# Linear attention plus gated MLP on one core: stage-by-stage kernel rewritten as one recorded plan for five engines

## The chip, the core and the metric

The kernel runs on one core of a Trainium2 chip. A core has TensorE (PE, matrix products; PEld is its weight load), VectorE (DVE), ScalarE (ACT), GpSimd (POOL) and SyncE (SP, which issues DMA). TensorE writes its results into PSUM; the other engines fetch them there. Both kernels divide PSUM into banks of 512 float32 columns, and the changed one uses eight.

The metric is device time in microseconds (us), lower is better. The kernel before took 369.79 us (median of all its 16 runs). The span of a profile is about 2 us less than the time of the same run. With one core there is no second die to compare with; all profiled runs quoted here are of the state "fast".

## The reference

x is 2048 tokens by 640. It is normalised once (xn); an attention block and a gated MLP both read xn, and x plus both is the output.

```python
xn = layernorm(x)
# A: 32 heads of 20; phi = [softmax(u), softmax(-u)] over the 20 features
q, k, v = split(xn @ wqkv)
phi_q, phi_k = phi(q @ w_phi), phi(k @ w_phi)
kv  = sum over tokens of phi_k^T v ;  z = sum over tokens of phi_k
o   = (phi_q @ kv) / (phi_q @ z + 1e-6)
A   = o @ wo
# B
h   = silu(xn @ w1) * (xn @ w3)          # 640 -> 1536
B   = h @ w2
return x + A + B
```

Every query needs the finished sum over all tokens, so A has a barrier in the middle. B (gate/up products, then output products) has none: it needs only xn. That freedom is what the change uses.

## The kernel before

Both kernels first fuse wq and wk with w_phi (transposes, then small products). The kernel before then does one stage after the other; the tile framework orders instructions inside a stage.

```python
nc.gpsimd.memset(vaug[:], 0.0)                 # 12096 columns
nc.gpsimd.memset(vaug[:, :, :, 120:126], 1.0)
... fuse wq, wk with w_phi (TensorE transposes, ScalarE copies) ...
for t in range(NST):                           # 16 tiles: all statistics first
    bn_stats, bn_stats, bn_aggr                # VectorE
rstd = ...                                     # one Sqrt for all 16 tiles
for t in range(NST): xn = ...; 5 transposes; copy to xnT
for t in range(NST): K and V products, exp, sums, reciprocals, phik, vaug
for g in range(NG): ... 16 KV products per group and sign ...
for sc in range(NSC):                          # 4 chunks of 512 tokens
    for g in range(NG):   pq = ...; eqp = exp(pq); eqm = exp(-pq)
    for tau in range(4):  rt, tt products; copies to r_sb, t_sb
    for fi in range(KF):                       # 12 gate/up blocks
        gp = 5 products; up = 5 products       # "bank_d"/"bank_e", "bank_f"
        th = tanh(gp / 2); up_sb = up / 2                        # ScalarE
        gs = (th + 1) * gp                                       # VectorE
        nc.gpsimd.tensor_mul(out=hT[:, fi, :], in0=gs[:], in1=up_sb[:])
    m1, m2, den, rinv, cB, cA                  # VectorE, attention arithmetic
    om1 = r * cB; om2 = t * cA; o = om1 + om2  # VectorE, 2880 columns each
    for tau in range(4):  transpose o -> oT
    for ti in range(4):   acc = hT @ w2 + oT @ wo; res = acc + xr; store
```

The softmax here doesn't subtract the row's maximum and nothing guards it: scores larger than these inputs give would overflow.

## Time and profile before

| | before |
|---|---|
| time, median | 369.79 us |
| span of the profile | 365.9 us |
| TensorE matmuls, columns | 2134, about 668,400 |
| columns / 2.4 GHz + 2.5 ns per matmul | about 284 us |
| span minus that | about 82 us |

The last rows need one reading: five back-to-back matmuls of 512 columns take 1.08 us in the chain of waits, 216 ns each, and sixteen of 126 columns take 0.88 us (their starts, 105.74 to 106.62 us), 55 ns each. Both are the columns / 2.4 GHz plus about 2.5 ns. Multiply out the code and one has an estimate of the time that TensorE needs at this pace without a pause, called its floor below. TensorE's "busy" is not that number, because the ends of matmuls are modelled.

The page's first two parts for the kernel before: busy time per engine, then forty slices of 9.1 us with the busy share in tenths.

```profile
PE 311.0 (85%) x2134; PEld 173.2 (47%) x2134; DVE 167.7 (46%) x294; ACT 175.5 (48%) x300; POOL 129.4 (35%) x93
...
PE   0006677999989999979999989999997999998885
...
PEclk9999969999999999989999999999999999999899
```

TensorE's row begins with three zeros and reaches 9 only in the eighth slice, and the clock row has a 6 in the sixth: TensorE had paused. The timeline of the first 60 us says why (start, duration, engine, line, operation, output<-inputs, count, in brackets the idle time before and what ended it).

```profile
8.89 1.28 DVE L166 BATCH_NORM_STATS2 stats<-xall 128x6 f32<-128x320 bf16 x3 [8.89 <-DMA xall<-in_A_x_dram]
...
9.79 10.20 POOL L115 MEMSET vaug<- 128x12096 bf16 x1
...
10.94 11.09 DVE L110 COPY selj<-ident 20x20 bf16<-20x20 bf16 x6
...
30.37 1.29 PE L141 MATMUL pwT<-ident,wq 128*120 128x128 bf16 x10 [0.42 <-DVE wphi L131]
...
48.24 6.11 PE L196 MATMUL pst<-ident,xn 128*128 128x128 bf16 x55 [2.20 <-DVE xn L186]
...
58.68 1.24 PE L219 MATMUL pk<-wkphi,xnT 128*128 128x512 bf16 x5 [1.35 <-ACT xnT L201]
```

At 9.79 us GpSimd starts to clear vaug for 10.2 us; VectorE's six small copies (20 columns each) take 11.09 us in that time, and the statistics behind them wait. The first fusion transpose is at 30.37 us, the first transpose of xn at 48.24, the first K product at 58.68.

The chain that ended last, as shares of the span by engine and by line:

```profile
PE 54%; POOL 12%; DVE 12%; issue 3%; ACT 2%; POOLq 1%; ACTq 0%
POOL hT L388 12%; PE acc L445 12%; PE gp L365 10%; PE up L373 10%; PE pq L331 8%; PE acc L453 6%; DVE sp L257 3%; DVE sm L260 3%; DVE phik_p L267 3%; PE kvp L294 3%; PE rt L345 2%; PE tt L355 2%; PE pot L433 1%; DVE rcm L266 1%; DVE res L46
```

Only 54% of what decided the end is TensorE. The largest single line is GpSimd's product hT. The timeline of the end of the first chunk:

```profile
145.68 12.95 POOL L388 TENSOR_TENSOR hT<-gs,up_sb 128x512 bf16<-128x512 bf16 x5 [0.89 <-ACT up_sb L383]
145.69 3.15 DVE L405 TENSOR_TENSOR om<-r_sb,cB 128x2880 bf16<-128x2880 bf16 x1
...
150.50 3.49 DVE L410 TENSOR_TENSOR om<-t_sb,cA 128x2880 bf16<-128x2880 bf16 x1
...
155.63 1.99 DVE L416 TENSOR_TENSOR o<-om,om 128x2880 bf16<-128x2880 bf16 x1
...
157.68 0.45 PE L433 MATMUL pot<-ident,o 128*128 128x128 bf16 x5 [1.76 <-DVE o L416]
```

Five hT products take 12.95 us there; alone one takes 1.15 us (the median of all 48). They run beside VectorE's three long attention products. The transposes of o wait for the last of these, and the output products for both.

### The profile page before, as it was taken

The page shows a single profiled execution, that of the slowest core. Times are in us where ns is not written, and L with a number is a line of the kernel's source. Part 1 is how long each engine was busy: PE and PEld are TensorE (multiplying, and loading weights), DVE is VectorE, ACT ScalarE, POOL GpSimd, SP SyncE. Part 2 cuts the span into 40 slices and gives each one's busy share as a digit, 9 for nine tenths or more (in the row PEclk, how much of TensorE's full clock was granted, in tenths as well). Part 3 has the DMA queues.
Part 4 walks back from the last instruction along what each step waited for, and adds up shares of the span by engine and source line. Part 5 has one row for each costly group of instructions (what it writes and reads, how often), then busy time and mean ns, then how long its engine had stood idle before and what let it go on. Part 6 is the DMA issues. An engine that isn't in the chain of part 4 may idle for free.

```text
span 365.9 us, 5348 instructions
## 1 busy us (share of the span) xinstructions
PE 311.0 (85%) x2134; PEld 173.2 (47%) x2134; DVE 167.7 (46%) x294; ACT 175.5 (48%) x300; POOL 129.4 (35%) x93
## 2 busy tenths in 40 slices
PE   0006677999989999979999989999997999998885
PEld 0005564555577445445545435554544554543442
DVE  0998072999962125921112780211394210279111
ACT  0006988877721777431177632237753216863300
POOL 7930000666630224930023690012386002359100
PEclk9999969999999999989999999999999999999899
DMA  8998000000010000002110001110000211000011
GB/s 246 370 390 289 2 0 3 0 2 0 3 39 2 0 0 2 1 0 73 37 37 0 2 0 36 56 53 3 1 0 2 68 42 36 2 0 0 27 47 36
DMA packets 13233, 17.39 MB, mean 48 GB/s; under 512 B 1690, under 2 KB 11930, under 8 KB 13210
## 3 DMA queue, kind: packets, MB, share of 16 engines
q1 hardware_dynamic: 9552, 13.76, 11.3%
q10 hardware_dynamic: 3274, 3.30, 2.8%
q8 instruction: 16, 0.26, 0.3%
q0 software_dynamic: 384, 0.01, 0.1%
q14 instruction: 7, 0.06, 0.1%
HBM read 14.44 MB, written 2.62 MB: 47 GB/s over the span
## 4 chain that ended last, share of the span: by engine, by line
PE 54%; POOL 12%; DVE 12%; issue 3%; ACT 2%; POOLq 1%; ACTq 0%
POOL hT L388 12%; PE acc L445 12%; PE gp L365 10%; PE up L373 10%; PE pq L331 8%; PE acc L453 6%; DVE sp L257 3%; DVE sm L260 3%; DVE phik_p L267 3%; PE kvp L294 3%; PE rt L345 2%; PE tt L355 2%; PE pot L433 1%; DVE rcm L266 1%; DVE res L463 1%
## 5 line engine op out<-in xcount | busy, mean ns | idle before, releaser
L388 POOL TENSOR_TENSOR hT<-gs,up_sb 128x512 bf16<-128x512 bf16 x48 | 83.8, 1758 | 150.6 <-ACT up_sb L383 144.9
L385 DVE SCALAR_TENSOR_TENSOR gs<-th,gp 128x512 bf16<-128x512 bf16 x48 | 32.8, 684 | 76.3 <-ACT th L381 72.6
L365 PE MATMUL gp<-xnT,w 128*128 128x512 bf16 x240 | 64.9, 380 | 0.6 <-DVE gs L385 0.5
L373 PE MATMUL up<-xnT,w 128*128 128x512 bf16 x240 | 63.7, 380 | 0.0
L445 PE MATMUL acc<-w,hT 128*128 128x512 bf16 (+1 forms) x384 | 60.2, 302 | 4.1 <-DVE res L463 2.7
L338 ACT ACTIVATE eqp<-pq 120x512 bf16<-120x512 f32 (+1 forms) x24 | 14.3, 596 | 70.6 <-PE pq L331 70.6
L463 DVE TENSOR_TENSOR res<-acc,xr 128x640 bf16<-128x640 f32 x16 | 13.2, 824 | 75.4 <-PE acc L453 75.4
L445 PEld LDWEIGHTS <-hT 128*128 128x128 bf16 x384 | 31.7, 100 | 30.2 <-issue 3.7
L272 POOL TENSOR_TENSOR phik_m<-ekm,rcm 128x640 bf16<-128x640 bf16 x16 | 26.1, 1631 | 43.7 <-PE vp L244 28.8
L383 ACT ACTIVATE up_sb<-up 128x512 bf16<-128x512 f32 x48 | 28.8, 600 | 18.0 <-POOL hT L388 10.2
L373 PEld LDWEIGHTS <-w 128*128 128x128 bf16 x240 | 22.3, 98 | 24.3 <-issue 0.4
L365 PEld LDWEIGHTS <-w 128*128 128x128 bf16 x240 | 22.0, 98 | 24.7 <-issue 3.0
L381 ACT ACTIVATE th<-gp 128x512 bf16<-128x512 f32 x48 | 28.7, 599 | 8.1 <-PE gp L365 7.9
L331 PE MATMUL pq<-xnT,wqphi 128*120 128x512 bf16 (+1 forms) x120 | 30.3, 379 | 0.8 <-DVE kvr_m L305 0.4
L453 PE MATMUL acc<-wo,oT 128*128 128x512 bf16 (+1 forms) x160 | 29.9, 315 | 0.0
L166 DVE BATCH_NORM_STATS2 stats<-xall 128x6 f32<-128x320 bf16 x32 | 23.5, 773 | 8.9 <-DMA xall<-in_A_x_dram 8.9
L126 PE MATMUL pwp<-wps,selj 20*120 20x120 bf16 (+1 forms) x6 | 1.3, 270 | 28.7 <-DVE stats L166 22.1
L219 PE MATMUL pk<-wkphi,xnT 128*128 128x512 bf16 x80 | 19.9, 379 | 1.4 <-ACT xnT L201 1.4
L436 ACT COPY oT<-pot 128x640 bf16<-128x640 bf16 x16 | 11.1, 692 | 20.6 <-PE pot L433 20.6
L236 PE MATMUL vp<-wv,xnT 128*128 128x512 bf16 x80 | 19.9, 379 | 0.0
L331 PEld LDWEIGHTS <-wqphi 128*120 128x120 bf16 (+1 forms) x120 | 14.4, 127 | 11.0 <-issue 3.0
L453 PEld LDWEIGHTS <-oT 128*128 128x128 bf16 x160 | 13.3, 101 | 8.7 <-issue 1.1
(85 smaller groups left out, 413.9 us busy)
## 6 DMA issues: line engine op xcount, KB each, us to landing
w<-in_B_w_dram SPq DMA_DIRECT2D x3, 1920.0 KB, 24.0
xall<-in_A_x_dram SPq DMA_DIRECT2D x2, 1280.0 KB, 11.5
xr<-in_A_x_dram SPq DMA_DIRECT2D x16, 160.0 KB, 2.3
out_dram<-res SPq DMA_DIRECT2D x16, 160.0 KB, 1.8
wq<-in_A_wqkv_dram ACTq DMA_DIRECT2D x1, 800.0 KB, 10.1
wk<-in_A_wqkv_dram ACTq DMA_DIRECT2D x1, 800.0 KB, 14.9
wv<-in_A_wqkv_dram ACTq DMA_DIRECT2D x1, 800.0 KB, 21.5
wo<-in_A_wo_dram ACTq DMA_DIRECT2D x1, 800.0 KB, 25.4
```

Source lines behind the costliest of these rows:

```text
L166: nc.vector.bn_stats(out=stats[:, t, i, :], in_=xall[:, t, i * 320 : (i + 1) * 320])
L219: nc.tensor.matmul(pk[:, 0:512], xnT[:, c, t * P : (t + 1) * P], wkphi[:, c, 0:512], start=(c == 0), stop=(c == KD - 1),)
L272: nc.gpsimd.tensor_mul(out=phik_m[:, t, :].rearrange("p (h d) -> p h d", d=Dh), in0=ekm[:].rearrange("p (h d) -> p h d", d=Dh), in1=rcm[:, ...
L331: nc.tensor.matmul(pq[:gw, :], wqphi[:, c, 120 * g : 120 * g + gw], xnT[:, c, s0 : s0 + 512], start=(c == 0), stop=(c == KD - 1),)
L365: nc.tensor.matmul(gp[:, :], w1[:, c, fi * P : (fi + 1) * P], xnT[:, c, s0 : s0 + 512], start=(c == 0), stop=(c == KD - 1),)
L373: nc.tensor.matmul(up[:, :], w3[:, c, fi * P : (fi + 1) * P], xnT[:, c, s0 : s0 + 512], start=(c == 0), stop=(c == KD - 1),)
L381: nc.scalar.activation(out=th[:], in_=gp[:], func=AF.Tanh, scale=0.5)
L383: nc.scalar.activation(out=up_sb[:], in_=up[:], func=AF.Copy, scale=0.5)
L385: nc.vector.scalar_tensor_tensor(out=gs[:], in0=th[:], scalar=1.0, in1=gp[:], op0=ALU.add, op1=ALU.mult)
L388: nc.gpsimd.tensor_mul(out=hT[:, fi, :], in0=gs[:], in1=up_sb[:])
L445: nc.tensor.matmul(acc[:, n0:n1], hT[:, fi, ti * P : (ti + 1) * P], w2[:, fi, n0:n1], start=(fi == 0), stop=False,)
L453: nc.tensor.matmul(acc[:, n0:n1], oT[:, c, ti * P : (ti + 1) * P], wo[:, c, n0:n1], start=False, stop=(c == KD - 1),)
```

## The change

The intent: keep TensorE at work from the first data to the last, with gate/up blocks of B wherever A would leave it idle. The rewrite is nearly total; this is its core.

```diff
-stage after stage, order inside a stage left to the tile framework
+class Plan:              # operations are recorded with engine, guessed duration, dependencies,
+    def run(self): ...   # buffers; TensorE and allocations keep the recorded order, the other
+                         # engines may take any of their next 80 operations that is ready first
+ringp = tile_pool(bufs=6, PSUM)          # one ring of six banks for everything but KV
+kva, kvb                                 # two banks that collect KV, tile by tile
-x in two loads of 1.3 MB; some weights on another queue at the same time
+x tiles 0 to 3 in four loads, then wv, a quarter of w1/w3, wk, ... in order of need
-nc.gpsimd.memset(vaug[:], 0.0)           # 12096 columns
+vaug: four small tiles, only the columns of ones set
-statistics of all 16 tiles, then one rstd
+statistics, rstd, xn per pair of tiles, ahead of use
+16 warm-up matmuls on the first x tile
+def fill(us): issue gate/up blocks until so many us of TensorE work have been added
+for t in range(16):
+    K(t); fill(1.6); V(t); fill(1.6); T(t + 4); KV(t - 2); part of the wq fusion
-6 Q groups of 120 rows, last of 40       # 5 groups of 128
-attention arithmetic per chunk (2880 columns), then its transposes
+RT(0); RT(1); ATT(0); fill(2.2)
+for i in range(8):                       # pairs of tiles, 1280 columns
+    RT(2*i + 2); RT(2*i + 3)             # next pair
+    OT(2*i); OT(2*i + 1)                 # this pair's transposes (for i = 0 after Q, not before)
+    ATT(i + 1)                           # next pair's arithmetic, VectorE
+    fill(4.4); every other pair: Q of the next chunk
+    O(2*i); O(2*i + 1)                   # this pair's output products and store
-hT on GpSimd for all 48 blocks           # GpSimd for 40, VectorE for 8
```

RT is the product of exp(q) with the KV sums, ATT the attention arithmetic, OT the transposes of its result, O the output products.

## The prediction

> **What bounds the kernel now.** TensorE, but in three pieces with gaps. The timeline has almost no matmul before 30 us: VectorE's first read of x ends its wait at 8.9 us, and from 10.9 us a statistics instruction and a copy stand for 11 us behind GpSimd's 10.2 us clearing of vaug. The weight fusion's first transpose is at 30.4 us, the normalised x transposes at 48.2 to 57 us, the first K product at 58.7 us. K/V (58.7 to 104 us) runs at 2.7 us a tile, TensorE at 98% and VectorE nearly as full (windows view). The KV sums take 105 to 115 us. Then four 512-row chunks take 60 us each (the last ends at 366). Within a chunk the chain of waits passes three times to GpSimd's hT product (12% of the span in all), whose 12 multiplies (1.76 us each) hold the output matmuls back, and to the attention tail before the oT transposes.
>
> **TensorE's own floor.** Five 512-column matmuls take 1.08 us in the chain of waits, i.e. columns/2.4 GHz + 2.5 ns. The Trainium skill ("TensorE: Matmul & The Clock Gate", "Wait — 56ns, not 53.3ns?") gives the same sum; the trace agrees. Counting columns from the code: before 668,600 columns in 2134 matmuls = 284 us; after 655,800 in 2092 = 278.5 us. So the change removes only 5 us of TensorE work (Q in 5 full groups instead of 6, narrower KV products), and even pays 16 warm-up matmuls. It must earn its gain by filling about 80 us of idle or waiting TensorE.
>
> **What moves.** x comes in 160 KB pieces, first in the queue; the 10 us clearing is gone; normalisation is per tile; gate/up products serve as filler in the fusion, K/V and attention stages from one six-bank PSUM ring; KV accumulates tile by tile; each engine's order is fixed by a planner.
>
> **Other engines, estimated from traced durations.** VectorE about 200 us in all. In K/V, per tile: K about 2.7, statistics 0.86, xn 0.45, copy from PSUM about 0.5, gates about 1.0 us: 5.5 us against 6.6 us of TensorE work. ScalarE about 160 us, GpSimd about 105 us. None exceeds TensorE, but VectorE has little slack in K/V.
>
> **The sum.**
> - First data about 3.5 us (a 160 KB load lands in 2.3 us in the list of DMA issues).
> - Cold clock in the warm-up: 2 us (the windows view shows 0.5 granted at 48 to 52 us).
> - TensorE work 278.5 us, plus 2 for 84-column products limited by weight loads, plus 1 for clock.
> - Waits 15 us: about 1 us for each of eight attention pairs, because eight short RT groups (0.17 us of matmul each) fill six banks faster than ScalarE copies them (about 0.42 us); the rest in the fusion, K/V, and the change to attention.
> - Tail 4 us: add and output load.
> - Outside the span 2 us (367.8 against 365.9).
>
> Total 308 us: 0.83 of before. Range 297 to 321. Faster by over 2%: 0.97; within 2%: 0.02; slower: 0.01.
>
> **What would show each step.** First matmul at 3 to 5 us, first V product near 9 us; matmuls starting nearly without gaps from there; the hT product gone from the chain of waits; TensorE at over 85% of the chain; TensorE idle behind ScalarE's copies of RT; granted clock at 0.98 or more; the 11 us VectorE stall gone.
>
> **What would make it wrong.** VectorE and GpSimd blocking each other in K/V, where xn copies and GpSimd products now overlap (10 to 20 us more). Weight loads in 768-byte rows arriving late, so that early filler waits. VectorE standing in order behind the last x piece, queued behind all weights (about 33 us). A lower granted clock once TensorE is dense. On the other side, if the six-bank ring hides the copies, 297 us.

## The result, and the profile after

| | before | after |
|---|---|---|
| time, median | 369.79 us | 297.05 us (296.55 to 297.52, 11 runs) |
| span of the profile | 365.9 us | 294.6 us |
| span minus TensorE's floor | about 82 us | about 16 us |

The ratio is 0.8039 (95% interval 0.8012 to 0.8067). It is the mean time of one kernel's fast runs over that of the other's in the same rounds, so not quite the ratio of the medians above. The output is correct.

The same lines of the page after the change (slices are now 7.4 us):

```profile
PE 285.3 (97%) x2092; PEld 176.9 (60%) x2092; DVE 192.7 (65%) x341; ACT 144.7 (49%) x316; POOL 94.2 (32%) x115
...
PE   5899999899999999999999999999999999999995
...
PEclk9999999999999999999999999999999999999999
```

TensorE is at 9 in all but four slices (the first two, the eighth and the last); the clock row has no dip. The chain that ended last:

```profile
PE 84%; DVE 9%; ACT 3%; issue 2%; DMA 1%
PE bank L505 29%; PE bank L741 18%; PE bank L339 13%; PE bank L745 7%; PE bank L593 6%; PE bank L636 3%; DVE stats L253 2%; DVE ks L387 2%; PE bank L712 2%; PE kva L314 2%; ACT eq L608 2%; DVE gs L526 1%; PE bank L317 1%; DVE xnT L325 1%; A
```

In the changed kernel all PSUM tiles are called bank, so go by lines: L505 is gate/up, L741 and L745 the output products, L339 K and V, L593 Q, L636 RT, L712 OT, L317 the transposes of xn. TensorE is 84% of the chain, and hT is gone from its head. The start and the first V and K products (timeline, TensorE):

```profile
3.08 5.62 PE L314 MATMUL kva<-xg,ident 128*128 128x512 bf16 x16 [3.08 <-DMA xg<-in_A_x_dram]
...
8.54 1.00 PE L317 MATMUL bank<-ident,xn 128*128 128x128 bf16 x15
...
10.72 0.45 PE L317 MATMUL bank<-ident,xn 128*128 128x128 bf16 x5 [1.18 <-DVE xn L296]
...
11.01 5.60 PE L339 MATMUL bank<-wv,xnT 128*128 128x320 bf16 x40
...
33.22 1.58 PE L339 MATMUL bank<-wkphi,xnT 128*128 128x320 bf16 x10
```

The first K product comes 25 us earlier than before (33.2 against 58.7), and by then six gate/up blocks are done as well. All that TensorE still waited for in the whole span, by the view of waits (us in total, times, longest):

```profile
PE kva L314 <- DMA xg<-in_A_x_dram: 3.1, 1, 3.1
PE bank L317 <- DVE xn L296: 1.2, 1, 1.2
PE bank L505 <- DVE xnT L325: 0.9, 1, 0.9
PE bank L636 <- ACT eq L608: 0.4, 1, 0.4
```

One more, of 0.2 us, is left out. The list is short, but starts show more. Three neighbouring groups in the attention stage:

```profile
228.44 1.56 PE L636 MATMUL bank<-kvr,eq 128*128 128x154 bf16 x24
230.03 0.80 PE L712 MATMUL bank<-ident,om 128*128 128x128 bf16 x10
230.74 4.48 PE L505 MATMUL bank<-xnT,w 128*128 128x512 bf16 x20
```

From 228.44 to 230.74 is 2.30 us, for 24 RT matmuls and 10 transposes whose columns need 1.38 + 0.56 = 1.94 us. So 0.36 us was lost per pair, though no idle time is shown. The single records say where: the two tiles' transposes start at 230.03 and 230.39 us and the next gate/up product at 230.74, each 0.05 us after one of ScalarE's copies of RT ends (229.98, 230.33, 230.69). TensorE waits for a bank of the ring.

The last five matmuls start from 290.51 us on, so the last columns end near 291.2. From the first matmul (3.08) that is 288.1 us; a recount of the columns gives 278.1 us. The 10 us between them, each from starts against columns: cold warm-up 2.0; transposes of tiles 0 to 3 1.35; K fusion 0.75; K/V with KV 1.7; the first two pairs' RT about 1.95; six later pairs 2.2.

### The profile page after: what moved, and what is told of

Its sections match the earlier page's. It is cut to its first block, busy times and chain, and to the rows that moved or that the text cites. A ratio compares the mean times of both kernels' runs of the same rounds, so it can differ in the third digit from the quotient of the medians.

```text
span 294.6 us, 5283 instructions
## 1 busy us (share of the span) xinstructions
PE 285.3 (97%) x2092; PEld 176.9 (60%) x2092; DVE 192.7 (65%) x341; ACT 144.7 (49%) x316; POOL 94.2 (32%) x115
## 4 chain that ended last, share of the span: by engine, by line
PE 84%; DVE 9%; ACT 3%; issue 2%; DMA 1%
PE bank L505 29%; PE bank L741 18%; PE bank L339 13%; PE bank L745 7%; PE bank L593 6%; PE bank L636 3%; DVE stats L253 2%; DVE ks L387 2%; PE bank L712 2%; PE kva L314 2%; ACT eq L608 2%; DVE gs L526 1%; PE bank L317 1%; DVE xnT L325 1%; ACT rt L644 1%
## 5 line engine op out<-in xcount | busy, mean ns | idle before, releaser
L505 PE MATMUL bank<-xnT,w 128*128 128x512 bf16 x480 | 109.6, 379 | 1.0 <-DVE xnT L325 0.9
L548 POOL TENSOR_TENSOR hT<-gs,up 128x512 bf16<-128x512 bf16 x40 | 52.9, 1324 | 147.0 <-DVE gs L526 104.9
L505 PEld LDWEIGHTS <-w 128*128 128x128 bf16 x480 | 46.7, 98 | 51.4 <-issue 1.4
L741 PE MATMUL bank<-w,hT 128*128 128x320 bf16 x384 | 57.4, 299 | 0.0
L741 PEld LDWEIGHTS <-hT 128*128 128x128 bf16 x384 | 37.5, 98 | 15.2
L521 ACT ACTIVATE th<-bank 128x512 bf16<-128x512 f32 x48 | 28.8, 600 | 26.6 <-PE bank L505 22.2
L339 PEld LDWEIGHTS <-xnT 128*128 128x128 bf16 x320 | 30.4, 98 | 13.1
L526 DVE SCALAR_TENSOR_TENSOR gs<-th,bank 128x512 bf16<-128x512 bf16 x48 | 32.1, 671 | 4.0 <-ACT th L521 3.9
L543 ACT ACTIVATE up<-bank 128x512 bf16<-128x512 f32 x40 | 23.9, 597 | 21.4 <-PE bank L505 21.4
L403 POOL TENSOR_TENSOR phik<-ek,kr 128x640 bf16<-128x640 bf16 x16 | 27.8, 1735 | 12.5 <-DVE kr L396 10.0
L745 PE MATMUL bank<-wo,oT 128*128 128x320 bf16 x160 | 27.0, 299 | 0.0
L339 PE MATMUL bank<-wkphi,xnT 128*128 128x320 bf16 x160 | 24.4, 299 | 0.0
L339 PE MATMUL bank<-wv,xnT 128*128 128x320 bf16 x160 | 23.9, 299 | 0.0
L593 PE MATMUL bank<-xnT,wqphi 128*128 128x512 bf16 x100 | 22.2, 379 | 0.0
L745 PEld LDWEIGHTS <-oT 128*128 128x128 bf16 x160 | 15.7, 98 | 6.1
```

The source lines that it names most:

```text
L339: nc.tensor.matmul(o["ps"][:], xnT[:, c, t * P : (t + 1) * P], w[:, c, 320 * half : 320 * half + 320], start=(c == 0), stop=(c == KD - 1),)
L403: eng.tensor_mul(out=phik_b[t][:, :, sgn, :], in0=box["ek"][:, sgn, :].rearrange("p (h d) -> p h d", d=Dh), in1=box["r"][:, sgn, :, None]. ...
L505: nc.tensor.matmul(o["ps"][:], w[:, k, fi * P : (fi + 1) * P], xs[:, k, :], start=(k == 0), stop=(k == KD - 1))
L521: nc.scalar.activation(out=box["th"][:], in_=og["ps"][:], func=AF.Tanh, scale=0.5)
L526: nc.vector.scalar_tensor_tensor(out=box["gs"][:], in0=box["th"][:], scalar=1.0, in1=og["ps"][:], op0=ALU.add, op1=ALU.mult)
L548: lambda: nc.gpsimd.tensor_mul(out=hT[c][:, fi, :], in0=box["gs"][:], in1=box["up"][:]),
```

## The experiments

Each is one kernel. The "a" runs take one thing out of the changed kernel, the "b" runs put one thing into the kernel before, the "c" runs try to beat both. Times are medians; "after" is 297.05 us. The runs come from three sessions on three chips, in which the kernel before ran too (medians 368.45, 370.20 and 369.77 us) but the changed kernel did not. A difference of 1 or 2 us from "after" is therefore believed only where the trace shows it as well.

### 1. No filler before attention

```diff
-fill issues gate/up blocks from the start
+fill does nothing until the Q products; then as before, and each chunk's
+missing blocks are issued just before its output products
```

> The changed kernel with one thing undone: no gate/up product is issued before the attention stage; all 48 then run there, each chunk's before its output products. Theory (the early stages are full only because gate/up products fill them): without them the K/V stage is bound by VectorE (about 69 of its 86 busy us between 32 and 140 us remain against about 47 us of TensorE work) and the fusion by its copies, so the kernel takes 315 to 325 us, 18 to 28 over 297, with TensorE well under 75% busy before the Q products. Rival (the early start and per-tile flow do it, filler only covers crumbs): at most 303 us.

Measured: 323.37 us (322.99 to 324.65, 4 runs), 26 us slower. Busy time by stretch (length, then PE, PEld, DVE, ACT, POOL busy with counts, granted clock, DMA share, GB/s), first of this run:

```profile
20.00:32.00 12.00, 5.63 (x41) 3.57 (x41) 11.75 (x30) 3.98 (x13) 5.70 (x9) 0.80 1.09 347
32.00:105.00 73.00, 60.75 (x585) 43.67 (x584) 61.39 (x102) 40.78 (x108) 25.55 (x19) 0.92 0.17 55
```

and of the changed kernel:

```profile
20.00:32.00 12.00, 11.95 (x96) 7.01 (x94) 11.57 (x32) 7.75 (x18) 8.54 (x13) 1.00 1.09 347
32.00:140.00 108.00, 107.08 (x799) 64.67 (x798) 85.83 (x117) 67.28 (x152) 57.26 (x44) 1.00 0.07 21
```

VectorE is full from 20 to 32 us in both (11.75 and 11.57 of 12), but without filler TensorE has only 5.63 us of work beside it in place of 11.95. From 32 us to the first Q product at 95.6 us VectorE stays at 91% (57.9 of 63.6 us). TensorE's two longest waits there, 5.9 and 6.4 us for xn, each follow a block of statistics on VectorE; with VectorE that full, a better order could have saved some 6 us from 32 us on at most (an estimate: its 5.7 us of idle time). The granted clock reads 0.80 and 0.92, and two stretches at half clock begin inside these two waits. In the changed kernel the first Q product starts at 143.7 us; less the 33 blocks of 2.16 us taken out that would be 72.5 us. So 23 of the 26 us are lost before attention. The theory holds in size; TensorE was 76% busy there (72.6 of 95.6 us), a little more than I wrote, partly because slow-clock matmuls count as busy.

### 2. No filler inside attention

```diff
+issue all blocks of chunks 0 to 2 before Q(0)
-fill(2.2), fill(4.4) between pairs
+the last 12 blocks in one lump at the sixth pair
```

> The changed kernel with gate/up filler taken out of the attention stage: 36 products before it, the last 12 in one lump after the tenth tile's attention. Rival (filler between pairs is what hides the attention arithmetic there): 8 us or more slower, 305 us or over. Theory (issuing RT and the arithmetic one pair ahead of the output products hides it, since 9.2 us of output products are longer than the about 7 us from RT to oT): 297 to 302 us, any loss at the first pair, which has no output products before it.

Measured: 298.90 us (298.72 to 300.02, 4 runs), 1.9 us slower. The waits that appear are at the first pair (0.41 us for its arithmetic, 0.84 us for a copy). Filler between the pairs is almost worthless once the look-ahead is there; filler before attention (run 1) is worth 26 us.

### 3. No look-ahead

```diff
-RT(next pair); OT(this); ATT(next); fill; Q; O(this)
+RT(this); ATT(this); OT(this); O(this); fill; Q
```

> The changed kernel with the one-pair look-ahead undone: RT, arithmetic, transposes and output products of the same pair follow each other; gate/up filler stays, after each pair's output products. Theory (look-ahead hides the arithmetic): about 7 us of idle TensorE before each of the eight pairs' transposes, plus a colder clock after each, so 345 to 370 us. Rival (filler anywhere in the stage is enough): under 310 us.

Measured: 371.85 us (370.97 to 372.65, 4 runs), 74.8 us slower and by its ratio 1.0107 (1.0045 to 1.0169) even a little slower than the kernel before. It issues the same instructions. The TensorE timeline of one pair:

```profile
206.59 1.94 PE L636 MATMUL bank<-kvr,eq 128*128 128x154 bf16 x24
215.81 1.25 PE L712 MATMUL bank<-ident,om 128*128 128x128 bf16 x10 [7.27 <-DVE om L695]
216.85 3.41 PE L741 MATMUL bank<-w,hT 128*128 128x320 bf16 x12
```

and the wait in total:

```profile
PE bank L712 <- DVE om L695: 58.0, 8, 7.3
```

Eight waits of 7.3 us are 58 us. After each the clock had dropped (mean 0.911 over the span against 0.999): the next twelve output matmuls take 2.7 to 3.41 us instead of 1.79. From the transposes to the second half tile of output products it is 5.6 us here (215.81 to 221.38), the longest of all, and 4.2 to 5.3 us in the others (in one of them filler comes between), against 2.9 after the change; over the eight pairs this adds about 15 us. Waits and cold clock together, 73 us, cover the loss. One step between was not tried: the same pair's filler (4.3 us) put into the wait, between arithmetic and transposes. So the 75 us are the worth of look-ahead against filler behind the output products, not against filler in the best place.

### 4 and 5. Recorded order on every engine, and what of it matters

```diff
-VectorE, ScalarE, GpSimd, SyncE: best of the next 80 operations
+each takes its operations in the order recorded
```

> The changed kernel with the planner's reordering taken out: every engine gets its instructions in the order in which the code records them (TensorE's order nearly unchanged). If the planner's order matters: VectorE does the statistics of tiles 4 to 15 before the first K sums and stands behind the last x piece (lands near 30 to 37 us), gates wait behind it, 303 to 315 us. Rival (the recorded order is already interleaved finely enough): within 1%, 294 to 300 us.

Measured: 334.01 us (332.24 to 335.04, 4 runs), 37 us slower. The direction is right; the size is more than I expected, and the reason I gave is wrong. VectorE's timeline:

```profile
38.70 0.88 DVE L253 BATCH_NORM_STATS2 stats<-xg 128x6 f32<-128x320 bf16 x2
...
50.66 1.43 DVE L387 TENSOR_REDUCE ks<-ek 128x64 f32<-128x1280 bf16 x1
...
54.05 0.80 DVE L296 TENSOR_SCALAR xn<-xg,mv,rstd 128x640 bf16<-128x640 bf16 x1
```

and TensorE's:

```profile
40.01 2.32 PE L505 MATMUL bank<-xnT,w 128*128 128x512 bf16 x10
54.91 0.71 PE L317 MATMUL bank<-ident,xn 128*128 128x128 bf16 x5 [12.57 <-DVE xn L296]
```

VectorE does the statistics of twelve tiles in one block, 38.7 to 50.6 us, with no wait for DMA among them: the data had landed. Tile 4's xn comes after that, and TensorE stands for 12.57 us. Then every tile waits 0.8 to 3 us, because xn is recorded right before the transposes that need it; TensorE waits 29.6 us for xn in all. So the next kernel keeps the recorded order and only records these two things earlier:

```diff
+statistics of tiles 4 to 7 before the K fusion, of later tiles eight tiles ahead
+xn(t + 4) before K(t)
-statistics of tiles 4 to 15 in one place; xn inside T
```

> The kernel of the run without reordering (recorded order on every engine), with only two things recorded earlier: the statistics of tiles 4 to 7 before the K fusion and of later tiles eight tiles ahead, and each xn before the K product of the tile four earlier. Theory from that run's trace (its 37 us are VectorE doing 12 us of statistics in one block ahead of tile 4's xn, then each xn recorded right before the transposes that need it, 1 to 3 us per tile, and the start, 3 us later): 300 to 308 us, the start's loss remaining. Rival (fine reordering of gates, sums and copies is what counts): 320 us or more.

Measured: 304.44 us (302.82 to 304.61, 4 runs).

```profile
14.21 8.06 PE L340 MATMUL bank<-wv,xnT 128*128 128x320 bf16 x40
...
40.81 1.58 PE L340 MATMUL bank<-wkphi,xnT 128*128 128x320 bf16 x10
```

Two moves recover 29.6 of the 37 us. The rest lies before the first K product (40.8 us here, 33.2 after the change; the first V product at 14.2 against 11.0). So the planner is worth 37 us over the order as written, but 7 us over an order that calls what TensorE needs early enough.

### 6. Four banks

```diff
-Plan(dict(bank=6, ...));  ringp = tile_pool(bufs=6)
+Plan(dict(bank=4, ...));  ringp = tile_pool(bufs=4)
```

> The changed kernel with four PSUM banks in the shared ring in place of six (the planner is told). Theory of the prediction, scaled down by what the trace shows (with six banks a pair's RT products lose only about 0.35 us): with four, the eight RT groups are paced by ScalarE's 0.37 us copies, about 1.2 us more per pair, and gate/up products in K/V wait for banks held by tanh and gate: 305 to 317 us. Rival (the ring has slack): at most 300 us.

Measured: 310.37 us (309.94 to 311.41, 4 runs), 13.3 us slower. A pair:

```profile
238.30 2.27 PE L636 MATMUL bank<-kvr,eq 128*128 128x154 bf16 x24
...
241.31 4.48 PE L505 MATMUL bank<-xnT,w 128*128 128x512 bf16 x20
```

RT and transposes now take 3.01 us where they took 2.30. That is 0.7 us per pair, not the 1.2 expected; over all eight pairs 5.7 us. The first Q product is 5 us later (148.7 against 143.7), lost before attention, and 2 us are new waits of later gate/up, Q and output products. The ring does bound RT, as the prediction had it, and six banks are enough to keep that small.

### 7. No warm-up

```diff
-for _ in range(16): matmul(kva, ident, xt(0)[:, 0:512])
+(none)
```

> The changed kernel without the 16 warm-up matmuls. Theory (they stand in time that TensorE would spend waiting for the first normalised tiles and for the V weights, which land near 10 us; without them the V products run at half clock[...]): the same to 2 us slower, 297 to 299.5 us. Rival, as the prediction's sum counted it (warm-up is 3.5 us of work plus 2 us of cold clock on the path): 292 to 294 us.

Measured: 298.34 us (297.88 to 299.12, 6 runs), 1.3 us slower, as the theory said. The intervals of the two ratios to the kernel before overlap (0.8049 to 0.8117, and 0.8012 to 0.8067), so the trace has to show it:

```profile
10.84 6.97 PE L339 MATMUL bank<-wv,xnT 128*128 128x320 bf16 x40
17.64 4.48 PE L505 MATMUL bank<-xnT,w 128*128 128x512 bf16 x20
```

The first V product starts at 10.84 us without warm-up, and between 10.5 and 11.1 us in the runs that have it (11.01 after the change; 14.2 where VectorE keeps the recorded order). Without it the 40 V products take 6.80 us until the next group (10.84 to 17.64), with it 5.43 (11.01 to 16.44): the 1.3 us. The Trainium skill ("TensorE: Matmul & The Clock Gate", Part 1) says that the clock is at half rate until about 3.4 us of sustained activity; the spacing after the change agrees roughly (0.43 us per 512 columns in the first 4.1 us, 0.216 later). The warm-up delays the first transposes (8.54 us, 7.61 without it), but not the V products, which wait for the fourth tile's xn in both.

### 8. The kernel before, with a smaller clearing

```diff
-nc.gpsimd.memset(vaug[:], 0.0)
+nc.gpsimd.memset(vaug[:, :, NG - 1, 40:120], 0.0)
```

> The kernel before with one line changed: GpSimd clears only the 80 unused columns of vaug's last group, not all 12096 columns (10.2 us). Theory (that clearing holds VectorE for 11 us and so the whole start): the 11 us VectorE stall is gone, the first transpose of the fusion moves from 30.4 to about 20 us, and the kernel takes 357 to 362 us. Rival (weights and x arrive too late for it to matter): 366 us or more.

Measured: 358.64 us (357.59 to 360.88, 4 runs), against 370.20 before in the same rounds. That median counts three slow runs; by the ratio of fast runs, 0.9722 (0.9662 to 0.9783), the gain is about 10 us.

```profile
10.20 1.19 POOL L115 MEMSET vaug<- 128x1280 bf16 x1
10.57 2.83 DVE L110 COPY selj<-ident 20x20 bf16<-20x20 bf16 x6
...
21.75 1.29 PE L141 MATMUL pwT<-ident,wq 128*120 128x128 bf16 x10 [0.42 <-DVE wphi L131]
```

VectorE's copies take 2.83 us instead of 11.09, and the first fusion transpose moves from 30.37 to 21.75 us. The Trainium skill ("SBUF — State Buffer", "Who interferes with whom") says that VectorE's copies, in the modes that use two ports, and GpSimd share a port pair that is held for a whole instruction. Both traces fit that; that these copies ran in such a mode is not shown. The single records add something: the first copy ends at 21.97 us, not when the clearing ends (19.99) but when the row of smaller clearings right behind it does (21.94), and here at 13.34 after 13.30. One line bought 3%.

### 9. The kernel before, with hT on VectorE

```diff
-nc.gpsimd.tensor_mul(out=hT[:, fi, :], in0=gs[:], in1=up_sb[:])
+nc.vector.tensor_mul(out=hT[:, fi, :], in0=gs[:], in1=up_sb[:])
```

> The kernel before with one line changed: the gate times up product goes to VectorE, not GpSimd. Theory (in each chunk VectorE's 3 us attention products hold back GpSimd's hT product, 4.2 us at most against 1.15 at best, and the output products wait for that): about 2 to 3 us less per chunk, 357 to 364 us. Rival (the chunk's tail is the attention chain itself; hT only fills the same wait): 366 us or more.

Measured: 361.91 us (360.90 to 363.05, 4 runs); by the ratio of fast runs, 0.9804 (0.9748 to 0.9860), about 7 us faster. From the first to the last Q matmul, three chunks, first before, then in this run (minimum, median, maximum ns of one, first and last start):

```profile
L331 PE MATMUL pq<-xnT,wqphi x120: 376/379/427, 115.2 to 309.1; 128*120 128x512 bf16 x100, 128*40 128x512 bf16 x20
```

```profile
L331 PE MATMUL pq<-xnT,wqphi x120: 376/379/427, 117.2 to 305.8; 128*120 128x512 bf16 x100, 128*40 128x512 bf16 x20
```

193.9 us become 188.6, 1.8 us per chunk. A chunk takes 60.0 us before (first transpose of o to that of the next chunk, 219.02 to 279.00), and its columns need an estimated 54.7 us. So the hT product at the head of the chain of waits was a real wait, but only about a third of the chunk's loss; in this run VectorE, with the attention products and hT, has 21% of the chain of waits in place of 12%. The same section of the skill says that a VectorE instruction with two SBUF inputs contends with a GpSimd instruction that reads SBUF. The trace agrees: hT takes 1.15 us alone and up to 4.18 us before, where it meets a VectorE product of 3.15 us; after the change, beside products of 1.48 us, it takes 2.27.

### 10. The kernel before, with both lines

> The kernel before with both one-line edits, the smaller clearing and the gate product on VectorE. If the two act in separate stages, their gains add: about 10 and 7 us, 350 to 353 us, still 53 us or more behind the changed kernel. Rival (one hides the other): 357 us or more.

Measured: 353.77 us (353.66 to 353.84, 4 runs) against 369.77 in its rounds; by the ratio of fast runs, 0.9587 (0.9550 to 0.9624), about 15 us, where 10 and 7 would add to 17. The intervals of the three ratios leave room for that difference, so the two gains add within the noise. It stays 57 us behind the changed kernel.

### 11 and 12. Two attempts to beat it

Once KV is summed, its two banks are free. The first attempt gives them to half of the RT groups; the second also normalises tiles 0 to 3 before copying their transposes.

```diff
-RT groups: all from the ring of six
+RT groups of the minus sign: the two KV banks (one bank per side)
+second attempt: copies of xnT for tiles 0 to 3 wait for xn(3)
```

> An attempt to beat the changed kernel: from the attention stage on, half of the RT groups use the two PSUM banks that held the KV sums, so RT has eight banks in all. If the six-bank ring is what stretches a pair's RT and transposes from about 1.9 to 2.3 us and the first two pairs by 1 us each: 2 to 4 us faster, 293 to 295 us. Rival (matmuls of 88 to 154 columns are slower than their columns for another reason, such as weight loads): no change, 296.5 to 297.5 us.

> The previous attempt, and in addition VectorE normalises all of tiles 0 to 3 before it copies their transposes, so that the fourth does not wait (it cost 1.2 us of TensorE at 9.5 to 10.7 us). If the V weights have landed by 10 us: 0.5 to 1.2 us faster than the previous attempt. Rival (V weights bind): no change.

Measured: 299.19 us (298.76 to 299.36) and 298.99 us (298.63 to 299.04), 4 runs each. Both are about 2 us slower than the changed kernel, and their ratios (0.8107, from 0.8080, and 0.8101, from 0.8075) lie above its interval. In the first, a pair looks like this:

```profile
231.07 0.47 ACT L647 CAST rt<-kva 128x352 bf16<-128x352 f32 x1
...
231.59 0.33 PE L639 MATMUL kva<-kvr,eq 128*128 128x154 bf16 x3 [0.39 <-ACT rt L647]
...
232.67 3.62 PE L505 MATMUL bank<-xnT,w 128*128 128x512 bf16 x16
```

The banks are not a common ring: the first tile's minus groups hold one each, and the second tile's minus groups need the same two 1.25 us later. They wait for ScalarE (0.39 us), and RT with transposes takes 2.67 us from 230.00 to 232.67, against 2.30. Eight banks bound to fixed users were worse than six shared ones. In the second attempt the gap between the third and fourth transposes is gone, and V starts at 10.52 us; but V starts vary between 10.5 and 11.1 us among runs, and by the first K product 0.15 us is left (33.13 against 33.28). Its gain is not resolved. Giving the KV banks only to the last two groups of a pair, so that each is used once per pair, was not tried.

## Why the prediction was right or wrong

The measured 297.05 us lies at the very edge of the stated range (297 to 321) and 11 us under the predicted 308. That it is inside owes something to luck: nearly every term below was put too high, so the errors added up instead of cancelling. The mechanism was right: TensorE's work hardly changes, the gain is filled idle time. The sum, term by term:

| term | predicted us | measured us |
|---|---|---|
| first data | 3.5 | 3.1 (first matmul at 3.08) |
| cold warm-up | 2 | 2.0 |
| TensorE's columns | 278.5 | 278.1 |
| 84-column products, clock | 2 + 1 | about 0 |
| waits | 15 | 8.0 |
| tail | 4 | 3.4 |
| outside the span | 2 | 2.4 (2.1 in the profiled run itself) |
| total | 308 | 297.0 |

- **"Waits 15 us" was the mis-sized term.** I put 1 us on each of eight pairs for RT. Six of them lost 0.36 to 0.40 us and the first two about 1 us each, 4.2 us in all; 0.4 us of the first pair's is a wait for an exponential of q, not for a bank. I had taken 0.42 us for a copy; eight run in 2.95 us, 0.37 each, and they start while RT is still running. That the mechanism is the right one is shown by the starts 0.05 us after the ends of copies, and by the four-bank run. The remaining waits I put at 7 us and they were 3.8.
- **"Plus 2 for 84-column products limited by weight loads" was wrong.** Ten KV products start within 0.38 us, 38 ns each, where columns / 2.4 GHz + 2.5 ns gives 37.5, with a weight load for every one.
- **"Plus 1 for clock" was not needed.** The granted clock is 0.999 (from 7.2 us on, where its records begin; the cold start is counted above), and TensorE was dense throughout.
- **What I feared did not happen.** VectorE is 79% busy in K/V (85.8 of 108 us) and its order leaves room. VectorE and GpSimd do lengthen each other (phik on VectorE takes 1.36 us on average and 0.81 at best), but none of TensorE's waits is for phik.
- **"VectorE standing in order behind the last x piece" named a real danger with the wrong cause.** In the run without reordering the 12 us are the statistics themselves, on data that was there.
- **"The first V product near 9 us" was 2 us early.** The fourth transpose waited for an xn that VectorE took after three copies.
- **The reading of the kernel before stands, with one weight shifted.** The clearing was worth about 10 us alone. hT, at the head of the chain of waits with 12% of the span (44 us), was worth about 7 us alone: a share of the chain is not a gain.

The parts do not add, so no run gives the share of each in the 73 us. What the runs show is what each is needed for: without look-ahead, and with filler only behind the output products, the whole gain is lost (75 us), without an order that calls VectorE's work early half of it (37), without early filler a third (26), with four banks a sixth (13), without filler in attention or without warm-up hardly any (1.9 and 1.3).

## What to carry to other kernels

Count the columns first: the distance between the span and TensorE's floor (82 us here) tells what an order of instructions can win at most, before one looks at any wait. Then give TensorE independent work in the stages where another engine is the bound, and issue each chain of small steps one unit ahead of its use; with look-ahead in place, filler in that stage adds almost nothing. Where an engine takes its instructions in the order recorded, record each one when its result must start to exist, not where it is consumed (37 us here, of which two such moves won back 29.6).

## What the Trainium skill lacked or had wrong

- "TensorE: Matmul & The Clock Gate", section "Back-to-back issue gap", gives about 81 ns for 128 columns and 131 ns for 512 for a sustained stream of weight loads and matmuls, and calls columns / 2.4 GHz + 2.5 ns the isolated gap. Here sustained streams with a weight load per matmul follow the latter: 216 ns at 512 columns, 136 ns at 320 (40 V products in 5.43 us), 38 ns at 84.
- No page says that the profile's granted clock reads 1.00 where it has no record: between 3.5 and 9 us it reads 1.00 after the change, but the first record begins at 7.2 us, and 512-column matmuls start 0.43 us apart until then and 0.216 us apart from there. In the kernel before the first record begins at 36.7 us. Until the first record, judge the clock by the spacing.
- "SBUF — State Buffer", section "Who interferes with whom", fits what contends here, and lacks a size for it in a kernel: 11.09 us instead of 2.83 for six 20-column copies beside a 10.2 us clearing, and 4.18 us at most for a 1.15 us GpSimd product beside VectorE products of 3.15 us. It also does not say that a row of GpSimd instructions without a gap can keep VectorE out until the last of them: the copies ended 0.03 and 0.04 us after such a row (21.97 after 21.94, 13.34 after 13.30).
